# v_m times w1 for four batches in one matmul: two row halves, a doubled w1, and pieces moved by DMA

## The chip, the cores and the metric

One core of a Trainium2 chip runs the kernel. The metric is the device time of one execution in microseconds (us). The kernel before took 1427.96 us (median of 3 runs, 1426.88 to 1429.84).

The engines named below: PE is TensorE (matmuls, with their weight loads PEld), DVE is VectorE, ACT is ScalarE, POOL is GpSimd. SP is the queue on which this kernel issues its DMAs. Each engine works through its own instructions in order and waits where one needs another engine's result. A line such as L446 is a line of the kernel that was profiled.

## What is computed

A memory-compressed attention over 8 batches of 8 heads (576 positions, head size 64, 32 memory slots), then a mixture of 4 experts over all 4608 rows:

```python
a = exp(phi - max(phi)); a = a / (a.sum(over positions) + 1e-9)
k_m = einsum('bhsm,bhsd->bhmd', a, k)
v_m = einsum('bhsm,bhsd->bhmd', a, v)
attn = softmax(q @ k_m^T / sqrt(64))         # 576 x 32 for a head
x = (attn @ v_m) as 4608 rows x 512
p = domain_probs / (domain_probs.sum(-1) + 1e-9)
for e in range(4):
    out += p[:, e:e+1] * (relu(x @ w1[e]) @ w2[e])   # w1: 512 x 1024, w2: 1024 x 512
```

Everything is float32. The large matmuls run in a rounded format (fp32r). A number is split in two: its rounded part (a copy on ACT, which rounds) and the remainder (a subtraction on DVE or POOL). A product then takes three matmuls: rounded x rounded, rounded x remainder, remainder x rounded.

## The kernel before

**The product is reassociated.** attn @ v_m @ w1 is worked out as attn @ (v_m @ w1): for each batch and expert, the 8 heads' v_m (32 slots each, 256 rows in all) are multiplied by their 64 rows of w1, which gives a matrix called vw of 256 x 1024. It stands in SBUF as four tiles a batch, [128 rows, 2 parts, 512 columns]: `fh` (0, 1) is the half of the 1024 columns, `g` (0, 1) a group of four heads, 32 rows for each head, and the 2 parts are rounded and remainder. The first layer then has 256 rows to contract over instead of 512.

**Loops.** Batches go in pairs, k = 0 to 3. A pair goes through four experts, an expert through 32 steps: the even batch's positions in two halves (256 and 320 columns) of 8 steps each, then the odd batch's (320 and 256). A step s has `first(s)`, six matmuls of vw with the transposed attention weights AT into one PSUM tile, a relu on ACT (L427) and the remainder on DVE (L429); and `second(s)`, six or nine matmuls of that h with w2 (L445 to L447). `first` runs two steps ahead of `second`. A pair thus has 128 steps, the whole 512.

**A passage** from one expert to the next is spread over the last dozen steps of an expert. Four loads of w2 and four of w1 come into the `stage` buffers (5 of 512 KB), are split (`split`, L118 and L119, ACT and DVE) and, for w1, feed `vw_mm`: for each of eight (fh, head pair), three matmuls into a PSUM tile `pv` (L364 to L366), with `vt` as the stationary operand. `vt` holds a pair of batches' v_m laid out so that 128 output rows are 2 batches x 2 heads x 32 slots. `vw_out` takes them out of PSUM, for each batch half the rows: a cast on ACT (L379) and a subtraction on DVE (L380). So a passage has 24 matmuls of 512 columns, 16 casts and 16 subtractions for vw.

**Attention work** of a later batch is a list of units (`att_units`): normalise phi, turn it, split k and v (`unit_kv`, four loads), fold them to k_m and v_m (`kv_pick` into `kvT`), write v_m into `vt` (`write_vt`), then scores, softmax and the transposes to AT. The two batches of pair k + 1 are worked through during pair k.

**What sets the order.** A plan written out by hand gives the step of every unit (`W2_AT`, `W1_AT`, `VW_AT`, the `UNITS_` tables). The recording layer then puts each engine's instructions into an order of its own, by when it thinks that each is ready. All DMAs are issued from SP, in order; `stage_ahead` issues loads as stage buffers come free. DMAs share eight semaphores in turn, so one waits for the one eight places before it. PSUM has four buffers `pm` for first layers, pv and attention, and four `p2` for the second layer. The opening (up to the first steps) is ordered by hand.

## Time and profile before

| | |
|---|---|
| time, median of 3 runs | 1427.96 us |
| the profiled execution: its time | 1428.84 us |
| its span, first to last instruction | 1427.1 us |
| granted TensorE clock, mean | 0.996 |
| matmuls | 7808 |
| DMA, SP's queue | 113.86 MB, 24.5% of 16 engines' span |

The profile is of one execution. Its page gives for each engine the busy time, then the span in slices, the chain of work that ended last, and groups of like instructions: busy time, mean ns of one, the idle time just before them and what ended it. Other views list the waits (who waited for whom), the instructions in order of time, the busy time in chosen stretches, and the DMAs with the time from issue to landing. Matmuls overlap in the pipeline, so the listed duration of one (0.39 us for 512 columns) is longer than the distance to the next.

### The profile page before, as it was taken

How to read it: one execution, taken by the hardware profiler on the slowest of the kernel's cores; microseconds unless marked ns; L12 is line 12 of the kernel's file. 1: busy time of each engine (PE TensorE's matmuls, PEld its weight loads, DVE VectorE, ACT ScalarE, POOL GpSimd, SP SyncE). 2: the span in 40 equal slices, each digit the busy share in tenths (PEclk: the TensorE clock that was granted, in tenths of full speed). 3: DMA queues.
4: the chain of work that ended last, by engine and by line, in shares of the span. 5: the costliest groups of instructions: out<-in, count | busy, mean ns of one | idle time of the engine just before them, and what ended most of it. 6: DMA issues, size and time to landing. Idle time of an engine off the chain costs nothing.

```text
span 1427.1 us, 20830 instructions
## 1 busy us (share of the span) xinstructions
PE 1412.3 (99%) x7808; PEld 1233.5 (86%) x7808; DVE 837.2 (59%) x1853; ACT 620.2 (43%) x1543; POOL 27.8 (2%) x27
## 2 busy tenths in 40 slices
PE   7999999999999999999999999999999999999998
PEld 6888888888888888888888888888888888888887
DVE  7876638666385654837547375573846446272722
ACT  6655426453263533635335362452625234161521
POOL 3300000000000000000000000000000000000000
PEclk8999999999999999999999999999999999999999
DMA  6632303323141120412214121140323103030001
GB/s 245 198 118 75 121 28 126 104 64 104 39 161 61 64 89 16 137 58 78 94 63 135 59 88 65 46 130 18 107 75 96 60 25 94 1 119 1 1 30 38
DMA packets 35957, 115.20 MB, mean 81 GB/s; under 512 B 3984, under 2 KB 5136, under 8 KB 35856
## 3 DMA queue, kind: packets, MB, share of 16 engines
q1 hardware_dynamic: 35856, 113.86, 24.5%
q8 instruction: 62, 1.02, 0.3%
q14 instruction: 39, 0.32, 0.1%
HBM read 104.41 MB, written 9.44 MB: 80 GB/s over the span
## 4 chain that ended last, share of the span: by engine, by line
PE 92%; DMA 2%; DVE 2%; ACT 2%; issue 1%; POOL 0%; SPq 0%; ACTq 0%
PE p L446 18%; PE p L447 18%; PE p L445 18%; PE p L415 9%; PE p L417 9%; PE p L416 9%; PE sc L304 2%; PE pv L366 2%; PE pv L364 2%; PE x L230 2%; PE pv L365 2%; DMA stage<-in_w 1%; PE tp L349 1%; PE kvp L249 1%; ACT w L118 0%
## 5 line engine op out<-in xcount | busy, mean ns | idle before, releaser
L446 PE MATMUL p<-w,h 128*128 128x512 f32 x1024 | 404.3, 395 | 0.0
L447 PE MATMUL p<-w,h 128*128 128x512 f32 x1024 | 402.8, 394 | 0.0
L445 PE MATMUL p<-w,h 128*128 128x512 f32 x1024 | 402.7, 393 | 0.0
L427 ACT ACTIVATE h<-p 128x256 fp32r<-128x256 f32 x512 | 195.2, 382 | 331.5 <-PE p L417 294.3
L429 DVE SCALAR_TENSOR_TENSOR h<-p,h 128x256 fp32r<-128x256 f32 x512 | 213.9, 418 | 206.3 <-ACT h L427 110.0
L415 PE MATMUL p<-AT,vw 128*128 128x256 f32 (+1 forms) x1024 | 308.2, 301 | 0.0
L417 PE MATMUL p<-AT,vw 128*128 128x256 f32 (+1 forms) x1024 | 304.3, 297 | 0.1
L416 PE MATMUL p<-AT,vw 128*128 128x256 f32 (+1 forms) x1024 | 303.6, 297 | 0.0
L447 PEld LDWEIGHTS p<-w,h 128*128 128x128 f32 x1024 | 192.4, 188 | 43.3 <-DVE nm L154 0.2
L119 DVE TENSOR_TENSOR w<-stage,w 128x512 fp32r<-128x512 f32 x259 | 175.9, 687 | 78.4 <-ACT w L118 77.1
L445 PEld LDWEIGHTS p<-w,h 128*128 128x128 f32 x1024 | 193.2, 189 | 23.3
L446 PEld LDWEIGHTS p<-w,h 128*128 128x128 f32 x1024 | 192.6, 188 | 22.0
L416 PEld LDWEIGHTS p<-AT,vw 128*128 128x128 f32 x1024 | 194.5, 190 | 19.5 <-DVE AT L356 0.3
L415 PEld LDWEIGHTS p<-AT,vw 128*128 128x128 f32 x1024 | 194.0, 189 | 19.1
L417 PEld LDWEIGHTS p<-AT,vw 128*128 128x128 f32 x1024 | 193.5, 189 | 0.7 <-DVE vw L380 0.6
L118 ACT CAST w<-stage 128x512 fp32r<-128x512 f32 x262 | 159.6, 620 | 79.1 <-DMA stage<-in_w 47.3
L380 DVE TENSOR_TENSOR vw<-pv,vw 64x512 fp32r<-64x512 f32 x254 | 172.1, 685 | 8.9 <-ACT vw L379 5.5
L429 DVE SCALAR_TENSOR_TENSOR hm<-p,hm 128x64 fp32r<-128x64 f32 x256 | 56.0, 219 | 201.9 <-ACT h L427 200.9
L379 ACT CAST vw<-pv 64x512 fp32r<-64x512 f32 x254 | 145.5, 580 | 58.5 <-DVE vw L380 42.6
L427 ACT ACTIVATE hm<-p 128x64 fp32r<-128x64 f32 x256 | 56.6, 221 | 227.9 <-PE p L417 227.9
L462 DVE SCALAR_TENSOR_TENSOR acc<-p,pt,acc 128x512 f32<-128x512 f32 x96 | 67.8, 741 | 2.6 <-PE p L447 2.6
L366 PE MATMUL pv<-w,vt 128*128 128x512 f32 x136 | 53.7, 395 | 0.0
(81 smaller groups left out, 1020.5 us busy)
## 6 DMA issues: line engine op xcount, KB each, us to landing
stage<-in_w SPq DMA_DIRECT2D x132, 512.0 KB, 3.8
stage<-in_kv SPq DMA_DIRECT2D x32, 512.0 KB, 4.1
stage<-in_qm SPq DMA_DIRECT2D x16, 512.0 KB, 3.7
out<-acc SPq DMA_DIRECT2D x32, 256.0 KB, 2.1
ph<-in_phi SPq DMA_DIRECT2D x16, 288.0 KB, 3.5
stage<-in_kvt SPq DMA_DIRECT2D x8, 512.0 KB, 3.8
stage<-in_qt SPq DMA_DIRECT2D x8, 128.0 KB, 3.2
out<-accm SPq DMA_DIRECT2D x4, 256.0 KB, 2.2
```

Source lines behind the costliest of these rows:

```text
L118: nc.scalar.copy(dst[:, 0, :], raw)
L119: eng.tensor_sub(dst[:, 1, :], raw, dst[:, 0, :].bitcast(F32))
L379: nc.scalar.copy(t[r, 0, :], ps[r])
L380: nc.vector.tensor_sub(t[r, 1, :], ps[r], t[r, 0, :].bitcast(F32))
L415: nc.tensor.matmul(ps, w[:, 0, f], at_t[:, g, 0, c], start=g == 0, stop=False)
L416: nc.tensor.matmul(ps, w[:, 0, f], at_t[:, g, 1, c], start=False, stop=False)
L417: nc.tensor.matmul(ps, w[:, 1, f], at_t[:, g, 0, c], start=False, stop=g == 1)
L427: nc.scalar.activation(t[:, 0, to], ps[:, at_], AF.Relu)
L429: nc.vector.scalar_tensor_tensor(t[:, 1, to], ps[:, at_], 0.0, t[:, 0, to].bitcast(F32), ALU.max, ALU.subtract)
L445: nc.tensor.matmul(po[t], x[:, 0, :], w[:, 0, :], start=j == 0, stop=False)
L446: nc.tensor.matmul(po[t], x[:, 0, :], w[:, 1, :], start=False, stop=False)
L447: nc.tensor.matmul(po[t], x[:, 1, :], w[:, 0, :], start=False, stop=j == NJ - 1)
```

## The change

For two groups of four batches (n = 0: batches 0 to 3, n = 1: batches 4 to 7), vw of a whole group is made at once: for n = 0 only for expert 3, for n = 1 for all four experts (`FOUR`). That happens in five passages; in the five that would have made the same for the group's second pair, finished tiles are loaded instead; the other five passages stay.

- `unit_four` takes one load of `w1d`, a copy of w1 made on the host in which the 64 rows of a head stand twice, on both halves of the 128 partitions. For each of two heads: cast on ACT, remainder on POOL, two matmuls (rounded and remainder of w1) with `vs` as the stationary operand. `vs` has for each head the rounded v_m on the upper 64 rows and its remainder on the lower 64, with 4 batches x 32 slots as the 128 output rows. So one matmul sums two products, and the remainder x remainder product is added.
- The result of a head (128 rows, 512 columns) is cast on ACT and its remainder taken on DVE into a tile `vst` (3 buffers, shared with `kvs`). Its rows belong to four batches: four DMAs of 32 rows and 128 KB move them, two into the vw tiles of the group's first pair, two into DRAM tiles `vwd` for the second. 16 heads in a passage make 64 such pieces.
- `load_vw` brings the second pair's tiles back (8 loads of 512 KB in a passage), one pair later.
- A row block of vst must keep its place, so batch b takes head h in slot h ^ TURN[b % 4] (the host permutes the heads).
- `kvT` is replaced by four `kT` and a small `v`; `vt` is kept for batches 0 to 3 alone; `kv_pick`, `write_vt` copy in smaller pieces; `v_hi`, `write_vs` are new. The k and v of all of batches 4 to 7 are worked out in pair 1 (table `ATT`), where those of 6 and 7 were made in pair 2.
- Buffers: stage 5 to 4, w2 10 to 9, kvs 2 to 3.

```diff
-STAGE = 5
-KVS = 2
+STAGE = 4
+KVS = 3
+VW_LOAD_AT = ((18, 22), (26, 30))
+TURN = (0, 2, 1, 3)
+FOUR = (3, 0)
+FOUR_AT = ((23, 24, 25, 27), (28, 29, 31, 32))
...
+KV_STEPS = (5, 5, 6, 8, 9, 12, 15, 18, 21)
+EVEN, ODD = (0, 4, 4, 8, 11, 11), (0, 5, 5, 10, 12, 13)
+ATT = {
+    2: (0, 31, (69, EVEN)), 3: (0, 61, (99, ODD)),
+    4: (PAIR, 0, (37, EVEN)), 5: (PAIR, 30, (99, ODD)),
+    6: (PAIR, 60, (PAIR + 37, EVEN)), 7: (PAIR, 88, (PAIR + 99, ODD)),
+}
...
-    kvT = [const.tile([P, 2, NP, 2 * M], F32, name=f"kvT{i}") for i in range(2)]
-    for t in kvT:
+    kT = [const.tile([P, NP, 2 * M], F32, name=f"kT{i}") for i in range(4)]
+    vts = [const.tile([P, NP, 2, P], F32R, name=f"vt{i}") for i in range(2)]
+    for t in [vts[0].bitcast(F32)] + kT + [vts[1].bitcast(F32)]:
         nc.gpsimd.memset(t, 0.0)
...
     def kv_pick(b, g):
...
+        for w in (1, 0):
+            for i in range(2):
+                r, m = slice(64 * i, 64 * i + 64), slice(M * i, M * i + M)
+                lo = slice(2 * M + M * i, 2 * M + M * i + M)
+                a = slice(2 * g, 2 * g + 2)
+                dst = st["v", b][r, a] if w else kT[b % 4][r, a, m]
+                src = st["kvp", b, g][r, :, w]
+                (nc.vector.tensor_copy if i else nc.scalar.copy)(dst, src[:, :, m])
+                nc.vector.tensor_add(dst, dst, src[:, :, lo])
...
+    def write_vs(b):
+        if b % 4 == 0:
+            st["vs", b // 4] = att.tile([P, 2, 4, P], F32R, name="vs", tag="vs")
+        vs, (v, vh) = st["vs", b // 4], v_hi(b, None)
+        for h in range(4):
+            q = slot(b, h)
+            rq, c = slice(64 * (q % 2), 64 * (q % 2) + 64), slice(M * q, M * q + M)
+            x, hi = v[rq, :, q // 2, :], vh[rq, :, q // 2, :]
+            if q % 2 == 0:
+                nc.scalar.copy(vs[:64, :, h, c], hi.bitcast(F32))
+            else:
+                nc.vector.tensor_copy(vs[:64, :, h, c], hi.bitcast(F32))
+            nc.vector.tensor_sub(vs[64:, :, h, c], x, hi.bitcast(F32))
...
+    def unit_four(n, e, fh, hp):
+        def emit(raw):
+            g, vs = hp // 2, st["vs", n]
+            for i in range(2):
+                h = 2 * (hp % 2) + i
+                w = wp.tile([P, 2, 512], F32R, name="w1", tag="w1", bufs=4)
+                split(w, raw[:, i, :], nc.gpsimd)
+                ps = psum.tile([P, 512], F32, name="pv", tag="pm", bufs=4)
+                for a in range(2):
+                    nc.tensor.matmul(ps, vs[:, g, h, :], w[:, a, :], start=a == 0, stop=a == 1)
+                t = att.tile([P, 2, 512], F32R, name="vst", tag="kvs", bufs=KVS)
+                nc.scalar.copy(t[:, 0, :], ps)
+                nc.vector.tensor_sub(t[:, 1, :], ps, t[:, 0, :].bitcast(F32))
+                for b in range(4):
+                    odd, r = b % 2, slice(M * slot(b, h), M * slot(b, h) + M)
+                    if b < 2:
+                        to = vw_tile(2 * n, e, odd, fh, g)
+                    else:
+                        if h == 0:
+                            key = f"vwd{n}{e}{odd}{fh}{g}"
+                            vwd[2 * n + 1, e, odd, fh, g] = dram.tile([P, 2, 512], F32, name=key)
+                        to = vwd[2 * n + 1, e, odd, fh, g]
+                    nc.sync.dma_start(to[r].bitcast(F32) if b < 2 else to[r], t[r].bitcast(F32))
+        return ("w1d", e, fh, hp), emit
+
+    def load_vw(k, e, odd, fh):
+        for g in range(2):
+            key = (k, e, odd, fh, g)
+            nc.sync.dma_start(vw_tile(*key).bitcast(F32), vwd.pop(key))
...
+                four = ne >= FOUR[nk // 2]
                 n = 0
                 for fh in range(2):
-                    for g in range(2):
+                    for hp in range(NP if four and nk % 2 == 0 else 0):
+                        at(s + FOUR_AT[fh][hp], unit_four(nk // 2, ne, fh, hp))
+                    for odd in range(2 if four and nk % 2 else 0):
+                        at(s + VW_LOAD_AT[odd][fh], lambda a=(nk, ne, odd, fh): load_vw(*a))
+                    for g in range(0 if four else 2):
                         at(s + W1_AT[2 * fh + g], unit_w1(nk, ne, fh, g))
...
+        "w1d": c(
+            np.tile(moe_w1.reshape(E, NP, 2, D, 2, 512).transpose(0, 4, 1, 3, 2, 5), (1, 1, 1, 2, 1, 1))
+        ),
```

Three places show how the instructions move. All are in the passage from the third to the fourth expert of pair 0, the first that makes vw for four batches. The numbers are those of tiles.

SP's queue, before: the loads of that passage, w2 and w1, and then queries.

```order
L104 DMA stage_2930<-in_w2 128x1024
L104 DMA stage_3023<-in_w1 128x1024
L104 DMA stage_3096<-in_w2 128x1024
L104 DMA stage_3126<-in_w1 128x1024
L104 DMA stage_3152<-in_w1 128x1024
L104 DMA stage_3186<-in_qm 128x1024
```

SP's queue now, some way into the passage: the pieces of head 3 (vst_3278), the loads of w1d for heads 6 and 7 (stage_3303) and for 8 and 9, and the pieces of head 4 (vst_3319).

```order
L473 DMA vw_3214<-vst_3278 32x1024
L473 DMA vw_3216<-vst_3278 32x1024
L473 DMA vwd03000_3218<-vst_3278 32x1024
L473 DMA vwd03100_3220<-vst_3278 32x1024
L123 DMA stage_3303<-in_w1d 128x1024
L123 DMA stage_3311<-in_w1d 128x1024
L473 DMA vw_3322<-vst_3319 32x1024
L473 DMA vw_3324<-vst_3319 32x1024
L473 DMA vwd03001_3326<-vst_3319 32x1024
L473 DMA vwd03101_3328<-vst_3319 32x1024
```

The loads for later heads now stand behind the pieces of earlier ones on one queue; before, nothing stood between loads.

PE, before: a head pair's three matmuls for two batches (pv), between the six matmuls of a second layer and a first layer.

```order
L445 MATMUL p2_3148<-w2_2075,h_3111 128x512
L446 MATMUL p2_3148<-w2_2075,h_3111 128x512
L447 MATMUL p2_3148<-w2_2075,h_3111 128x512
L364 MATMUL pv_3176<-w1_3128,vt_123 128x512
L365 MATMUL pv_3176<-w1_3128,vt_123 128x512
L366 MATMUL pv_3176<-w1_3128,vt_123 128x512
L415 MATMUL p1_3194<-AT_966,vw_2350 128x256
L416 MATMUL p1_3194<-AT_966,vw_2350 128x256
```

PE now: the end of 18 matmuls of second layers (the last two are shown), heads 6 and 7 with two matmuls each for four batches, a first layer, and heads 8 and 9.

```order
L532 MATMUL p2_3299<-w2_2273,h_3366 128x512
L533 MATMUL p2_3299<-w2_2273,h_3366 128x512
L460 MATMUL pv_3388<-w1_3385,vs_404 128x512 x2
L460 MATMUL pv_3401<-w1_3398,vs_404 128x512 x2
L501 MATMUL p1_3411<-AT_1020,vw_2429 128x256
L502 MATMUL p1_3411<-AT_1020,vw_2429 128x256
L503 MATMUL p1_3411<-AT_1020,vw_2429 128x256
L501 MATMUL p1_3411<-AT_1020,vw_2489 128x256
L502 MATMUL p1_3411<-AT_1020,vw_2489 128x256
L503 MATMUL p1_3411<-AT_1020,vw_2489 128x256
L460 MATMUL pv_3432<-w1_3429,vs_404 128x512 x2
L460 MATMUL pv_3449<-w1_3446,vs_404 128x512 x2
```

Heads come in twos, and a step's second layer no longer stands between one pv and the next.

ACT now, where the casts of the load for heads 12 and 13 stand (stage_3383): they are ahead of a relu (h_3510) and of head 9's cast (vst_3452).

```order
L137 CAST w1_3477<-stage_3375 128x512
L137 CAST w1_3490<-stage_3375 128x512
L137 CAST w1_3537<-stage_3383 128x512
L137 CAST w1_3554<-stage_3383 128x512
L513 ACTIVATE h_3510<-p1_3503 128x256
L462 CAST vst_3452<-pv_3449 128x512
```

ACT before, at the like place: casts of vw, of weights and relus take turns.

```order
L379 CAST vw_3246<-pv_3276 64x512
L118 CAST w1_3315<-stage_3152 128x512
L427 ACTIVATE h_3291<-p1_3284 128x256
L379 CAST vw_3249<-pv_3276 64x512
L118 CAST w2_3215<-stage_3096 128x512
L379 CAST vw_3304<-pv_3300 64x512
```

What moved is that casts for heads some way ahead stand together in front of work that earlier heads need.

More of the change, by code (lines that the diff above doesn't have):

```diff
@@ L69, in body @@
 @with_exitstack
-def body(ctx: ExitStack, tc: tile.TileContext, qm, qt, kv, kvt, phi, prob, w1, w2, out):
+def body(ctx: ExitStack, tc: tile.TileContext, qm, qt, kv, kvt, phi, prob, w1, w1d, w2, out):
     nc = tc.nc
@@ L134, in emit @@
             for i in range(2):
-                t = wp.tile([P, 2, DM], F32R, name="w2", tag="w2", bufs=NJ + 2)
+                t = wp.tile([P, 2, DM], F32R, name="w2", tag="w2", bufs=NJ + 1)
                 split(t, raw[:, i, :], eng)
@@ L253, in kv_pick @@
     def kv_pick(b, g):
-        kvd = kvT[b % 2][:, :, 2 * g:2 * g + 2]
-        kvp = st["kvp", b, g].rearrange("p h w c -> p w h c")
-        for i in range(2):
-            r, m = slice(64 * i, 64 * i + 64), slice(M * i, M * i + M)
-            if i == 0:
-                nc.scalar.copy(kvd[r, :, :, m], kvp[r, :, :, m])
-            else:
-                nc.vector.tensor_copy(kvd[r, :, :, m], kvp[r, :, :, m])
-        for i in range(2):
-            r, m = slice(64 * i, 64 * i + 64), slice(M * i, M * i + M)
-            lo = slice(2 * M + M * i, 2 * M + M * i + M)
-            nc.vector.tensor_add(kvd[r, :, :, m], kvd[r, :, :, m], kvp[r, :, :, lo])
+        if g == 0:
+            st["v", b] = att.tile([P, NP, M], F32, name="v", tag="v", bufs=2)
+        for w in (1, 0):
[7 more added lines that the diff above has]
+                nc.vector.tensor_add(dst, dst, src[:, :, lo])
     def unit_kv(b, hp):
@@ L279, in unit_kv, with slot, v_hi, write_vt @@
         return ("kv", b, hp), emit
[L281 to L291 removed]
+    def slot(b, h):
+        return h ^ TURN[b % 4]
+    def v_hi(b, gs=slice(0, 2)):
+        if ("vh", b) not in st:
+            st["vh", b] = att.tile([P, NP, M], F32R, name="vh", tag="vh")
+        split = lambda t: t.rearrange("p (g a) m -> p g a m", g=2)
+        v, vh = split(st["v", b]), split(st["vh", b])
+        if gs is not None:
+            nc.scalar.copy(vh[:, gs], v[:, gs])
+        return v, vh
+    def write_vt(b, gs=slice(0, 2)):
+        v, vh = v_hi(b, None)
+        vt = vts[b // 2].rearrange("p (g a) s c -> p g a s c", g=2)
+        for h in range(4):
+            q = slot(b, h)
+            r, rq = (slice(64 * (i % 2), 64 * (i % 2) + 64) for i in (h, q))
+            dst = vt[r, gs, h // 2, :, M * q:M * q + M]
+            x, hi = v[rq, gs, q // 2, :], vh[rq, gs, q // 2, :]
+            if r == rq:
+                nc.scalar.copy(dst[:, :, 0, :], x)
+                hi = dst[:, :, 0, :]
+            else:
+                nc.vector.tensor_copy(dst[:, :, 0, :], hi.bitcast(F32))
+            nc.vector.tensor_sub(dst[:, :, 1, :], x, hi.bitcast(F32))
+    def write_vs(b):
+        if b % 4 == 0:
+            st["vs", b // 4] = att.tile([P, 2, 4, P], F32R, name="vs", tag="vs")
+        vs, (v, vh) = st["vs", b // 4], v_hi(b, None)
+        for h in range(4):
+            q = slot(b, h)
+            rq, c = slice(64 * (q % 2), 64 * (q % 2) + 64), slice(M * q, M * q + M)
[5 more added lines that the diff above has]
+            nc.vector.tensor_sub(vs[64:, :, h, c], x, hi.bitcast(F32))
     def tiles(t0):
@@ L297, in scores_mm @@
         nt, n = tiles(t0)
-        kvd = kvT[b % 2]
+        kvd = kT[b % 4]
         if hps[0] == 0:
@@ L474, in att_units, with write @@
         u += [unit_kv(b, hp) for hp in range(NP)]
-        u += [lambda: write_vt(b)]
+        def write():
+            v_hi(b)
+            if b < 4:
+                write_vt(b)
+            write_vs(b)
+        u += [write]
         u += [unit_scores(b, t0) for t0 in (0, 2, 4)]
@@ L626, in body @@
         probabilities()
+    v_hi(0)
+    write_vs(0)
     load_phi(1)
@@ L641, in slots @@
     def slots(a):
-        return np.stack([a[b] if b % 2 == 0 else a[b][[2, 3, 0, 1, 6, 7, 4, 5]] for b in range(B)])
+        heads = lambda b: [i ^ TURN[b % 4] for i in range(H)]
+        return np.stack([a[b][heads(b)] for b in range(B)])
     q, k, v, phi = slots(q), slots(k), slots(v), slots(phi)
```

77 lines of the change are left out of this document (34 added, 43 removed).

## The prediction

> **What bounds the kernel now.** I read the busy table of the page first, then the chain that ended last, then what TensorE (PE) waited for, and then stretches of the span.
>
> ```profile
> span 1427.1 us, 20830 instructions
> ...
> PE 1412.3 (99%) x7808; PEld 1233.5 (86%) x7808; DVE 837.2 (59%) x1853; ACT 620.2 (43%) x1543; POOL 27.8 (2%) x27
> ...
> PE 92%; DMA 2%; DVE 2%; ACT 2%; issue 1%; POOL 0%; SPq 0%; ACTq 0%
> ```
>
> PE is busy for 99% of the span and carries 92% of the chain. Busy alone doesn't say that PE sets the pace, so next come its waits (waiter, what it waited for, us in all, times, longest) and then two stretches (busy us of PE, weight loads, DVE, ACT, POOL, and last the clock and the DMA share), the opening and a passage from one expert to the next.
>
> ```profile
> PE x L230 <- DVE a L188: 2.7, 1, 2.7
> ...
> PE sc L304 <- PE x L233: 0.3, 1, 0.3
> ```
>
> ```profile
> 0.00:30.00 30.00, 21.30 (x120) 19.07 (x121) 21.57 (x43) 19.51 (x44) 14.11 (x17) 0.89 0.75 274
> 300.00:340.00 40.00, 40.00 (x225) 34.99 (x224) 31.24 (x59) 24.23 (x51) 0.00 (x0) 1.00 0.33 100
> ```
>
> The waits are the ends of a list of seven; the longest of all is 2.7 us. In the opening 30 us PE is busy for 21.3; in the passage it is busy for 40.00 of 40, while DVE has 31 us of work and ACT 24. After the opening, PE doesn't wait. So fewer matmuls shorten the span one for one, as long as no new wait appears.
>
> **What goes.** A matmul's listed duration overlaps its neighbours; its price is the distance between starts.
>
> ```profile
> 303.15 0.39 PE L365 MATMUL pv<-w,vt 128*128 128x512 f32 x1
> 303.38 0.40 PE L366 MATMUL pv<-w,vt 128*128 128x512 f32 x1
> 303.61 0.28 PE L415 MATMUL p<-AT,vw 128*128 128x256 f32 x1
> 303.73 0.28 PE L416 MATMUL p<-AT,vw 128*128 128x256 f32 x1
> ```
>
> That is 0.23 us for 512 columns (303.38 to 303.61) and 0.12 for 256. A passage now has 24 of the former. The change replaces two passages (2 x 24 = 48) by one with 16 heads x 2 = 32: 16 fewer, five times (last expert of the first four batches, all four of the others). 80 x 0.23 = **-18.4 us**.
>
> **The opening.** PE waits there, so longer chains count.
>
> ```profile
> L259 ACT COPY kvT<-kvp 64x128 f32<-64x128 f32 x16 | 4.1, 259 | 9.0 <-PE kvp L249 9.0
> ...
> L265 DVE TENSOR_TENSOR kvT<-kvT,kvp 64x128 f32<-64x128 f32 x32 | 9.1, 285 | 1.0
> L261 DVE COPY kvT<-kvp 64x128 f32<-64x128 f32 x16 | 4.7, 294 | 24.5 <-ACT kvT L259 24.4
> ...
> L291 DVE TENSOR_TENSOR vt<-kvT,vt 128x64 fp32r<-128x64 f32 x4 | 0.7, 223 | 0.3 <-ACT vt L290 0.3
> 8.71 1.27 POOL L219 TENSOR_TENSOR kvs<-stage,kvs 128x512 fp32r<-128x512 f32 x1 [6.52 <-ACT kvs L218]
> ```
>
> The pick of the second half had one copy on DVE (0.29) and two additions (0.57) ahead of the scores; now it has v and then k, six instructions of half the width, some 0.23 each by the 64-column row: 1.4, so 0.5 more. Two more subtractions for vt stand ahead of the maximum: 0.45. Together **+1.0 us** (between 0 and 2). Clearing three times the columns costs POOL about 2 us more, inside the 6.5 us that it idles before 8.71. The later small copies, and the k and v of batches 6 and 7 made one pair earlier, load DVE and ACT while PE has its slack of two steps; I cost them at nothing. If that cover fails, one step, 6 x 0.12 + 6 x 0.23 = 2.1 us, is the most that I would expect to see.
>
> So without any new wait: 1428.84 (the profiled execution, span plus 1.7 around it, 0.9 above the median of the runs shown) - 18.4 + 1.0 = 1411.4.
>
> **What is added: five windows.** In each, 16 heads go w1 half (ACT), remainder (POOL), two matmuls, cast (ACT), remainder (DVE), four pieces (SP's queue), and PE needs the first piece of the last head when the next expert begins. PE's order is the same in all five: head 6 stands 51 wide and 24 narrow matmuls after head 0 (14.6 us), head 7 0.46 later, head 8 1.64 after head 6, head 9 0.46 after that, and the last vw tile is wanted 113 wide, 78 narrow and 8 score matmuls after head 0, at 36.2 us. The durations that fill this, first of the engines:
>
> ```profile
> L119 POOL TENSOR_TENSOR w<-stage,w 128x512 fp32r<-128x512 f32 x3 | 3.8, 1287 | 6.2 <-ACT w L118 6.2
> ...
> L427 ACT ACTIVATE h<-p 128x256 fp32r<-128x256 f32 x512 | 195.2, 382 | 331.5 <-PE p L417 294.3 <-issue 32.9
> ...
> L379 ACT CAST vw<-pv 64x512 fp32r<-64x512 f32 x254 | 145.5, 580 | 58.5 <-DVE vw L380 42.6 <-PE pv L366 10.3
> ...
> L380 DVE TENSOR_TENSOR vw<-pv,vw 64x512 fp32r<-64x512 f32 x254 | 172.1, 685 | 8.9 <-ACT vw L379 5.5
> ...
> L118 ACT CAST w<-stage 128x512 fp32r<-128x512 f32 x262 | 159.6, 620 | 79.1 <-DMA stage<-in_w 47.3 <-PE p L447 28.6
> ```
>
> Then SP's issues (start, duration), two of a run and one alone, and the landings, over the whole span and, from the packets' row on, in the first 20 us alone:
>
> ```profile
> 2.12 0.43 SPq L104 DMA_DIRECT2D stage<-in_kvt  x1
> 2.59 0.43 SPq L104 DMA_DIRECT2D stage<-in_kv  x1
> ...
> 310.51 0.33 SPq L104 DMA_DIRECT2D stage<-in_qt  x1
> ```
>
> ```profile
> stage<-in_w SPq DMA_DIRECT2D x132, 512.0 KB, 3.8
> ...
> ph<-in_phi SPq DMA_DIRECT2D x16, 288.0 KB, 3.5
> ...
> out<-acc SPq DMA_DIRECT2D x32, 256.0 KB, 2.1
> ...
> DMA packets 2132, 6.72 MB, mean 336 GB/s; under 512 B 228, under 2 KB 356, under 8 KB 2132
> ...
> q1 hardware_dynamic: 2132, 6.72, 92.6%
> ...
> stage<-in_w SPq DMA_DIRECT2D x7, 512.0 KB, 7.5
> ```
>
> No row shows a DMA of 32 rows, so three prices have two ends each. *An issue*: 0.33 us by itself, 0.47 from start to start in a run (2.12 to 2.59); the pieces come in runs, so 0.47. *A piece's landing*: 2.1 (a write from SBUF) to 3.5 (a load of 288 KB); I take 2.8. *A load's landing*: 3.8, or 7.5 in the first 20 us, where the DMA engines are 92.6% busy at 336 GB/s, that is 363 at full share. A window moves 64 x 128 KB and some 8 loads of 512 KB, 12.6 MB: 35 us of the 36 by that rate, so a load won't land in 3.8 always; the queue isn't full from the start of a window, and I take 5, nearer to 3.8. Each DMA of the queue also waits for the one eight before it; eight issues take 3.8 us, so this binds only where landings are longer.
>
> A head's tile is ready 0.46 + 0.58 + 0.69 = 1.7 us after its matmuls begin; four pieces take SP 1.9. From head 0's matmuls: its pieces 1.7 to 3.6, head 1's to 5.5, a load to 6.0, head 2's to 7.9. There are three tile buffers, so head 3 waits for head 0's last piece (issued 3.1, landed 5.9), is ready at 7.2, and its pieces go out till 9.8. Only then SP issues the load for heads 6 and 7: landed 14.8, cast 15.4, POOL 16.7. PE wants it at 14.6: **2.1 late**. Head 7's remainder follows at 18.0 (0.8 late again), head 8's at 19.3 (0.1), head 9's at 20.6 (0.8): POOL makes one each 1.29 us, where PE's order has them in pairs. That is 3.8. Then the tail: the load for heads 12 and 13 needs the buffer of heads 6 and 7 (18.0), lands at 23.0, and its casts stand on ACT ahead of a relu and head 9's cast: 23.0 + 1.24 + 0.38 + 0.58 + 0.69 = 25.9. From there 28 pieces and 3 loads take 14.6 us, to 40.5; the last head's first piece went out at 38.6 and landed at 41.4, and PE wants it at 36.2 + 3.8 = 40.0: 1.4. **5.2 us a window, 26 in all: 1411.4 + 26 = 1437 us.**
>
> With the cheap ends (0.33, 2.1, 3.8) the load for heads 6 and 7 goes out at 8.1, the remainder is there at 13.8, and only the pairs cost, 0.9 a window: 1416. With the dear ends (0.47, 3.5, 7.5) head 6 is 4.6 late, the pairs cost 1.7, the tail 4.6, 10.9 in all: 1466. What is also dear: DVE's subtraction of two SBUF operands beside POOL.
>
> ```profile
> L614 DVE TENSOR_TENSOR w<-stage,w 128x512 fp32r<-128x512 f32 x2 | 2.2, 1135 | 0.0
> ```
>
> 1.135 us beside a busy POOL; there are eight such for w2 in a window, off the chain of heads, so I leave them in the range.
>
> The order speaks for waits too, though not for their length: before, each pv triple stands behind a plain step; now 18 matmuls of the second layer stand together ahead of head 6, which was not ready for an earlier place.
>
> **Rivals.** *The windows hold* (not slower). Place: the load for heads 6 and 7 behind 16 pieces. Price: 0.9 to 2.8 a window, 1416 to 1425. It decides at 3.5 a window, where 5 x 3.5 eats 17.4: with my landings, an issue of about 0.42 us. For it: one issue lasts 0.33 and a piece has a quarter of a load's rows. Against: DMA demand near the full rate.
>
> [...] If pieces move at half rate and one after another, a piece takes 128 KB at half of 418 GB/s, 0.63 us; 418 is the commonest full value in the opening 20 us, half a microsecond to a number:
>
> ```profile
> GB/s 0 0 0 111 115 383 364 371 295 336 189 156 164 336 352 401 426 418 418 401 451 410 418 418 418 434 410 401 418 410 410 377 399 398 388 413 415 395 410 410
> ```
>
> 64 x 0.63 + 8 loads x 1.25 = 50 us instead of 36; the last needed piece is three from the end, 1.7 + 50 - 1.9 + 2.1 = 52, so 16 late: 1411 + 80 = 1491. All transfers of this trace have 128 rows, so it neither shows nor excludes this. [...]
>
> *The change does not do what it says*: excluded by the order, which has 160 + 168 pv matmuls where there were 408.
>
> **Chances.** Forecast (waits of 3.9 to 11 a window): 0.37. Windows hold: 0.32. Between the two, within 0.2% (2.9 us, about what a measurement here can tell from no change): 0.13. Half rate: 0.18. So faster 0.32, same 0.13, slower 0.55. The range goes from 1414 (a little under the cheap end) to 1476 (over the dear end, leaving out most of the half-rate case).
>
> **What would show it.** In PE's waits after the change, pv of heads 6 to 9 behind POOL, or first layers behind DMA vw, five times, 3 to 6 us each time. Wrong would be: SP issues 0.33 to 0.42 us apart in the windows and loads landing under 4 us (windows hold); pieces landing in 4 us or more with issues waiting on earlier DMAs (half rate); PE waits outside the five windows (my zero for the moved attention work).

## The result, and the profile after

| | before | after |
|---|---|---|
| time, median (us) | 1427.42 (1426.48 to 1429.84, 4 runs) | 1568.05 (1564.17 to 1570.70, 4 runs) |
| ratio, 95% interval | | 1.0984 [1.0970, 1.0998] |
| span of the profiled execution (us) | 1427.1 | 1568.5 |
| mean granted TensorE clock | 0.996 | 0.953 |

Slower was right, by 10% instead of 0.6%: 1568 us against 1437 predicted, far above the range's end of 1476. The page of the changed kernel (busy time of the engines; PE and the granted clock in 40 slices; share of the chain that ended last):

```profile
PE 1455.6 (93%) x7728; PEld 1251.1 (80%) x7728; DVE 762.7 (49%) x1797; ACT 577.5 (37%) x1495; POOL 131.0 (8%) x111
...
PE   7999999978999999999977968977968999999999
...
PEclk8999999978999999999988978978978999999999
...
PE 83%; DMA 5%; DVE 4%; issue 3%; SPq 2%; ACT 2%; POOL 1%; DVEq 0%; POOLq 0%; ACTq 0%
```

PE dips at five places, the five windows, and its clock dips with it. 80 matmuls fewer, yet PE is busy for 43 us longer than the 1412.3 before. What PE waited for (waiter, what it waited for, us in all, times, longest):

```profile
PE pv L460 <- ACT w L137: 32.5, 10, 5.3
PE p L501 <- DMA vw<-vst: 13.8, 3, 7.8
...
PE p L501 <- DVE vst L463: 9.5, 4, 2.8
PE pv L460 <- POOL w L138: 8.3, 12, 0.9
```

Both waits that I named are there, but POOL's is the small one. The long ones are the copy of w1 that came late (ACT w) and the last heads' data at the start of the next expert (DMA vw, DVE vst).

In the second window the first head's matmuls start at 773.8. The matmuls of heads 6, 10 and 11, and the first layer that needs the last tile (start, duration, in brackets the wait before it):

```profile
792.83 0.79 PE L460 MATMUL pv<-w,vs 128*128 128x512 f32 x1 [4.28 <-ACT w L137]
...
804.21 0.50 PE L460 MATMUL pv<-w,vs 128*128 128x512 f32 x1 [1.71 <-ACT w L137]
805.56 0.80 PE L460 MATMUL pv<-w,vs 128*128 128x512 f32 x1 [0.85 <-POOL w L138]
...
837.26 0.55 PE L501 MATMUL p<-AT,vw 128*128 128x256 f32 x1 [7.75 <-DMA vw<-vst]
```

From head 0 to that first layer PE needs 63.5 us (773.8 to 837.26) for work that I put at 36.2. The same window in stretches (busy us of PE, weight loads, DVE, ACT, POOL; then the clock, the DMA share and GB/s):

```profile
774.00:786.00 12.00, 12.00 (x65) 10.29 (x64) 7.49 (x13) 5.88 (x13) 2.56 (x2) 1.00 0.73 199
788.50:792.50 4.00, 0.06 (x1) 0.00 (x0) 1.97 (x4) 1.93 (x4) 0.00 (x0) 0.93 0.94 305
792.50:798.50 6.00, 5.11 (x13) 3.56 (x14) 1.12 (x2) 2.90 (x6) 4.98 (x4) 0.50 0.93 272
798.50:802.50 4.00, 4.00 (x20) 3.06 (x18) 1.09 (x3) 1.49 (x3) 0.00 (x0) 0.97 0.84 246
802.50:806.00 3.50, 0.94 (x3) 0.63 (x3) 1.92 (x4) 3.18 (x6) 1.76 (x2) 0.94 0.54 133
806.00:809.50 3.50, 3.02 (x10) 1.91 (x10) 0.18 (x1) 0.59 (x2) 3.21 (x3) 0.57 0.87 238
```

Two things are to be seen. In five of the six stretches the DMA engines are 0.73 to 0.94 busy while they move 199 to 305 GB/s; the opening of before moved 336 at 0.926. And after PE has stood still for 4.28 us its clock is 0.50 over the next 6 us: 13 matmuls in 6 us, then 20 in 4.

The chain that ended last shows how a delay is handed on (start, duration, what; same window):

```profile
794.99 0.42 SPq L473
...
795.45 5.09 DMA stage<-in_w1d
...
804.24 1.28 POOL w L138
...
815.46 5.64 DMA stage<-in_w
821.12 0.62 ACT w L137
...
824.17 0.57 ACT vst L462
824.76 0.70 DVE vst L463
...
832.23 5.03 DMA vw<-vst
```

SP's pieces stand ahead of a load of w1d (5.09 us), which lands at 800.54. Its casts (heads 10 and 11, with those of 12 and 13 behind) start only 3 us later, because ACT has other casts ahead of them in its order; those of w2 had waited for matmuls of a second layer (L533), which were late themselves. ACT's casts of weights (start, duration of one or of four, in brackets the wait before them; the first two are of w2, the last four of w1d):

```profile
801.18 0.62 ACT L137 CAST w<-stage 128x512 fp32r<-128x512 f32 x1 [0.77 <-PE p L533]
...
802.54 0.62 ACT L137 CAST w<-stage 128x512 fp32r<-128x512 f32 x1 [0.26 <-PE p L533]
...
803.54 2.18 ACT L137 CAST w<-stage 128x512 fp32r<-128x512 f32 x4
```

The chain gives these 3 us to no one ("issue", 3.59 us before POOL). Later a load of w2 (5.64 us, `stage<-in_w`) holds up ACT, in whose order its cast stands ahead of a head's cast (vst), and that head's pieces are behind it again.

### The profile page after: what moved, and what is told of

Same layout as the page of the kernel before. It is cut to its first block, busy times and chain, and to the rows that moved or that the text cites. A ratio compares the mean times of both kernels' runs of the same rounds, so it can differ in the third digit from the quotient of the medians.

```text
span 1568.5 us, 21385 instructions
## 1 busy us (share of the span) xinstructions
PE 1455.6 (93%) x7728; PEld 1251.1 (80%) x7728; DVE 762.7 (49%) x1797; ACT 577.5 (37%) x1495; POOL 131.0 (8%) x111
## 4 chain that ended last, share of the span: by engine, by line
PE 83%; DMA 5%; DVE 4%; issue 3%; SPq 2%; ACT 2%; POOL 1%; DVEq 0%; POOLq 0%; ACTq 0%
PE p L531 16%; PE p L532 16%; PE p L533 16%; PE p L501 9%; PE p L503 8%; PE p L502 8%; PE sc L354 2%; SPq L473 2%; PE pv L460 2%; DMA stage<-in_w1d 2%; PE x L249 2%; DMA vw<-vst 1%; DMA stage<-in_w 1%; DVE vst L463 1%; PE pv L414 1%
## 5 line engine op out<-in xcount | busy, mean ns | idle before, releaser
L531 PE MATMUL p<-w,h 128*128 128x512 f32 x1024 | 411.4, 402 | 9.9 <-ACT h L513 9.9
L532 PE MATMUL p<-w,h 128*128 128x512 f32 x1024 | 409.1, 399 | 0.0
L533 PE MATMUL p<-w,h 128*128 128x512 f32 x1024 | 407.4, 398 | 0.7 <-DVE nm L173 0.7
L501 PE MATMUL p<-AT,vw 128*128 128x256 f32 (+1 forms) x1024 | 315.7, 308 | 33.8 <-DMA vw<-vst 13.8
L502 PE MATMUL p<-AT,vw 128*128 128x256 f32 (+1 forms) x1024 | 309.6, 302 | 0.8 <-DVE AT L406 0.8
L503 PE MATMUL p<-AT,vw 128*128 128x256 f32 (+1 forms) x1024 | 310.2, 303 | 0.2
L501 PEld LDWEIGHTS p<-AT,vw 128*128 128x128 f32 x1024 | 200.8, 196 | 57.5 <-issue 16.7
L533 PEld LDWEIGHTS p<-w,h 128*128 128x128 f32 x1024 | 195.9, 191 | 44.5 <-DVE nm L173 0.9
L531 PEld LDWEIGHTS p<-w,h 128*128 128x128 f32 x1024 | 196.5, 192 | 39.4 <-ACT h L513 14.7
L502 PEld LDWEIGHTS p<-AT,vw 128*128 128x128 f32 x1024 | 201.2, 196 | 21.3 <-DVE AT L406 1.3
L532 PEld LDWEIGHTS p<-w,h 128*128 128x128 f32 x1024 | 195.9, 191 | 23.0
L503 PEld LDWEIGHTS p<-AT,vw 128*128 128x128 f32 x1024 | 200.3, 196 | 0.8 <-DVE vw L435 0.5
L138 POOL TENSOR_TENSOR w<-stage,w 128x512 fp32r<-128x512 f32 x83 | 105.7, 1299 | 1006.2 <-ACT w L137 805.0
L138 DVE TENSOR_TENSOR w<-stage,w 128x512 fp32r<-128x512 f32 x179 | 122.7, 697 | 81.3 <-ACT w L137 79.3
L460 PE MATMUL pv<-w,vs 128*128 128x512 f32 x160 | 65.2, 505 | 48.6 <-ACT w L137 32.5
L460 PEld LDWEIGHTS pv<-w,vs 128*128 128x128 f32 x160 | 34.9, 231 | 71.5 <-ACT w L137 36.8
L463 DVE TENSOR_TENSOR vst<-pv,vst 128x512 fp32r<-128x512 f32 x80 | 53.3, 686 | 47.8 <-ACT vst L462 42.3
```

The source lines that it names most:

```text
L138: eng.tensor_sub(dst[:, 1, :], raw, dst[:, 0, :].bitcast(F32))
L460: nc.tensor.matmul(ps, vs[:, g, h, :], w[:, a, :], start=a == 0, stop=a == 1)
L463: nc.vector.tensor_sub(t[:, 1, :], ps, t[:, 0, :].bitcast(F32))
L501: nc.tensor.matmul(ps, w[:, 0, f], at_t[:, g, 0, c], start=g == 0, stop=False)
L502: nc.tensor.matmul(ps, w[:, 0, f], at_t[:, g, 1, c], start=False, stop=False)
L503: nc.tensor.matmul(ps, w[:, 1, f], at_t[:, g, 0, c], start=False, stop=g == 1)
```

## The experiments

Theories at the start: **A**, 32-row transfers hold the DMA engines longer than their bytes ask; **B**, SP's issues of 64 pieces set the pace; **D**, POOL's remainders in series; later **F**, the tail, from the last head to the next expert's first layer. In all runs "the change" is the changed kernel, of which one thing is altered. Where no number of runs stands beside a time, it is of one run.

### 1. Everything but the windows

```diff
-FOUR = (3, 0)
+FOUR = (4, 4)
```

(With a third `vt` tile, write_vt for all batches, and without write_vs.)

> Everything of the change but the four-batch passages: every expert's weights again by 24 narrow-row matmuls for each pair, the new order of the heads, the separate v tiles, the earlier attention work and the three kvs buffers stay. The recorded working (+1.0 us for the opening, nothing for the moved work): 1427 to 1431 us, like the kernel before. The rival that the moved attention work costs PE its slack: 2 us or more for each moved step, 1440 us and above.

**1438.26 us** (4 runs), ratio 1.0081 [1.0061, 1.0101] to 1426.57 before: +8.7 to +14.4 us, over the 1427 to 1431 expected, and not 1440 and above. The first matmul of the second layer starts at 36.38 us, 34.56 before: 1.8 us for the opening, within my 0 to 2 (the change itself has it at 36.57: 2.0). The other ten or so are spread over the run, with no single wait of PE over 2.2 us; whether the earlier attention work or the fewer buffers make them was not separated.

This gives a base for a window: 1438.3 - 18.4 = 1419.9 us without any window's cost. The price of a window in each run below is (its time - 1419.9) / 5; the change itself has 29.6 us.

### 2. The shape and the number of the transfers, and the tail

```diff
-                    odd, r = b % 2, slice(M * slot(b, h), M * slot(b, h) + M)
+                    odd, part, c = b % 2, h // 2, slice(256 * (h % 2), 256 * (h % 2) + 256)
...
-                    nc.sync.dma_start(to[r].bitcast(F32) if b < 2 else to[r], t[r].bitcast(F32))
+                    to = to[:, part, c]
+                    nc.sync.dma_start(to.bitcast(F32) if b < 2 else to, t[:, part, c].bitcast(F32))
```

> As the change, but each of a head's four pieces is a 128-row, 256-column block of one part of the tile instead of 32 rows of both parts: the same number of DMAs, the same 128 KB each, the same queue and order (the data lands in the wrong places, so the output is not the reference's). Theory A (32-row transfers hold the DMA engines longer than their bytes): the DMA share in the windows falls from 0.9 to about 0.75 at the same bytes, pieces land in 2 to 3 us, and the time falls to 1430-1470 us. Theory B (the issues on SP's one queue, four for a head at 0.58 us, set the pace): issues and time stay, 1545-1570 us.

**1501.18 us**, 16.3 a window: between the two theories, nearer to A's side in what it shows: same number of issues, the DMA share 0.72 in a window's stretch (755 to 790; 0.81 in the like stretch of the change, 773.8 to 809), and almost half of the cost gone. One sign of A did not come: the median landings are 3.7 and 2.9 us, not 2 to 3, and longer than the 3.3 and 2.5 of the change.

One DMA for a head (`b = h`, the whole tile t to one tile; the first pair's two tiles are those of heads 0 and 1 of each four):

> As the change, but one 128-row DMA of the whole 512 KB tile for each head instead of four pieces of 32 rows: a quarter of the DMAs, the same bytes (data in the wrong places, as in the run before). A and B both: no stall for pieces; 1411 plus what POOL's remainders cost, 1416-1425 us. Theory D (POOL's remainders of 1.3 us in series make most of a window's cost): 1500 us or more, with pv still behind POOL.

**1444.78 us**, 5.0 a window, 20 us over A and B's upper end, 8.5 of it the rest that the first run shows (1419.9 instead of 1411.4); far from D's 1500.

The same two with the last head's data needed first, as in the change:

```diff
-                b = h
+                b = 3 - h
```

> As the run with one 128-row DMA for a head, but in reverse: the last head of each four fills the first pair's even tile, which the next expert needs first (there it was the first head; data in the wrong places, as there). So PE again needs the last head's data at the start of the next expert, with 16 DMAs a window instead of 64. Theory F (the tail: last head, cast, remainder, transfer, first layer, is a large part of a window): 5 to 9 us more a window than with the first head, 1470-1490 us, with PE p waiting on DMA vw<-vst and the clock dropping there. If the tail is small (1.4 us a window, as the recorded working has it): 1445-1455 us.

**1480.72 us**, 12.2 a window: theory F as expected, 7.2 us more for nothing but the order. PE's waits of this run (the same columns as above):

```profile
PE p L499 <- DMA vw<-vst: 15.5, 4, 5.8
PE pv L460 <- POOL w L138: 10.4, 20, 1.1
```

```diff
-                    odd, part, c = b % 2, h // 2, slice(256 * (h % 2), 256 * (h % 2) + 256)
+                    odd, part, c = b % 2, (3 - h) // 2, slice(256 * ((3 - h) % 2), 256 * ((3 - h) % 2) + 256)
```

> As the run with pieces of 128 rows and 256 columns, but with the blocks in reverse, so that the first layers need the last head's pieces as they do in the change. Same number, bytes, queue and tail as the change; only the shape of a piece differs (data in the wrong places). Theory A (the 32-row shape costs): it stays near the 1501 us of the run before, under 1520. Theory F (its gain was the relaxed tail): 1540-1570 us.

**1502.59 us**, 16.5 a window: the gain of 128 rows is the shape's, not a relaxed tail's. So four kernels and the base make a ladder:

| step | time (us) | a window | the step's part |
|---|---|---|---|
| the change: 64 pieces of 32 rows, late tail | 1568.05 | 29.6 | |
| 64 pieces of 128 rows, late tail | 1502.59 | 16.5 | 13.1 shape |
| 16 DMAs of 128 rows, late tail | 1480.72 | 12.2 | 4.4 number and size |
| 16 DMAs of 128 rows, early tail | 1444.78 | 5.0 | 7.2 tail |
| no window (the first run, less 18.4) | 1419.9 | 0 | 5.0 the rest |

The third row has fewer DMAs, each four times as large and with whole rows, so its 4.4 us is not of the number alone. The parts hold for this order of steps; the three rows between are of one run each, and another order might share them out differently.

PE's busy rows of these kernels, from one late DMA for a head to 64 pieces of 128 rows, each of its own page:

```profile
PE 1424.0 (96%) x7728; PEld 1227.4 (83%) x7728; DVE 764.2 (52%) x1797; ACT 575.9 (39%) x1495; POOL 133.7 (9%) x111
```

```profile
PE 1435.9 (96%) x7728; PEld 1236.5 (82%) x7728; DVE 765.2 (51%) x1797; ACT 579.1 (39%) x1495; POOL 133.1 (9%) x111
```

and of the one with the early tail:

```profile
PE 1408.9 (98%) x7728; PEld 1216.3 (84%) x7728; DVE 763.2 (53%) x1797; ACT 575.7 (40%) x1495; POOL 134.0 (9%) x111
```

The same 7728 matmuls keep PE busy for 1408.9, 1424.0, 1435.9 and (the change) 1455.6 us, at mean clocks of 0.996, 0.982, 0.976 and 0.953. Of the 125.5 us of span between the first and the last, 46.7 are slower matmuls and 78.8 idle time: over a third of the price is the clock's. The clock by itself says the same: over stretches of 2 us, PE's busy time multiplied by what its clock lacks to 1 adds up to 52.3 us in the change and 4.6 in the kernel with the early tail, 47.7 more.

### 3. Bytes and issues

```diff
-                    nc.sync.dma_start(to[r].bitcast(F32) if b < 2 else to[r], t[r].bitcast(F32))
+                    nc.sync.dma_start(to[r, 0].bitcast(F32) if b < 2 else to[r, 0], t[r, 0].bitcast(F32))
```

(the first layers read part 0 twice, and the loads of `vwd` bring part 0 alone)

> As the change, but a piece carries only the rounded part of its 32 rows, 64 KB instead of 128, and the first layers read the rounded part in the place of the remainder: the same number of DMAs and the same rows, half the bytes. Theory A with a rate by bytes: DMA share in the windows near 0.6, landings under 3 us, 1430-1460 us. Theory B: issues stay at about 0.58 us each and the time at 1540-1570 us.

**1520.85 us**, 20.2 a window: half the bytes at the same number of pieces is worth 9.4 us a window. A's signs came (DMA share 0.62 in a window's stretch, 764 to 820; median landings 2.7 and 1.9 us), but not its time (1430 to 1460), and the time is under B's. Neither theory alone gives this.

```diff
-                for b in range(4):
+                for b in range(2):
```

> As the change, but the second pair's 32 pieces of each expert are left out, and its tiles are loaded from one DRAM tile written once (so the second pairs' outputs are wrong): SP issues 32 pieces a window instead of 64, some 23 us with the loads instead of 40, and the DMA engines move 8.4 MB instead of 12.6, 30 us at the 282 GB/s that full share gave in the window of the changed kernel. Both are under PE's 36 us. If issues and DMA time together make the cost: 1440-1455 us, as with one DMA for a head. If the 32-row copies from SBUF to SBUF alone are what is slow, whatever their number: landings of 3.3 us and more stay, and over 1480 us.

**1530.96 us**, 22.2 a window: a miss for both theories as I had put them, since half the issues and half of the pieces' bytes left three quarters of the cost. In this run the longest waits are the tail's (p on DMA vw: 16.1 us in three, up to 8.2), which it leaves in place. The other outcome, copies of 32 rows that are slow whatever their number, fits in its time (over 1480) but not in its sign: the median landing fell from 3.3 us to 2.7.

```diff
-                    nc.sync.dma_start(to[r].bitcast(F32) if b < 2 else to[r], t[r].bitcast(F32))
+                    q = nc.sync if b < 2 else nc.scalar
+                    q.dma_start(to[r].bitcast(F32) if b < 2 else to[r], t[r].bitcast(F32))
```

> As the change, but the second pair's 32 pieces are issued by ACT instead of SP. SP then issues for some 23 us a window, the DMA engines still carry 12.6 MB. Issues alone (theory B): 1440-1460 us. DMA time alone (theory A, 44.7 us at 282 GB/s against PE's 36): 1470 us or more, DMA share in the windows still 0.9. Rival for both: ACT stands in its order before each piece until DVE has made the remainder, so relu and casts come late: PE p <- ACT h grows from 9.9 us in all to over 40, 1540 us or more.

**1562.45 us**, 28.5 a window. Issues alone (1440 to 1460) are out. The rival's sign and its time (1540 or more) are there; A's bound (1470 or more) holds too, so the time doesn't tell these two apart. PE's longest waits:

```profile
PE p L532 <- ACT h L514: 41.6, 20, 5.1
PE pv L460 <- ACT w L137: 30.8, 11, 5.2
```

PE waits for the w1 copy as long as before (30.8 against 32.5), but now ACT comes late itself: its own waits for loads of w1d fell from 31.2 us in all to 9.9, while its casts of heads wait 33.5 us for the first pair's pieces (DMA vw<-vst; 0.3 in the change). The loads hardly go out sooner, the first 14.1 us after head 0's matmuls in the second window instead of 14.6, for they still stand behind pieces of heads that are late. The tail's wait (p on DMA vw) fell from 13.8 us to 0.8, and the one for relu grew from 9.9 to 41.6. So this run moves cost to ACT; it does not show that SP's issues cost nothing.

```diff
-            nc.sync.dma_start(t, src)
+            (nc.gpsimd if order[i][0] == "w1d" else nc.sync).dma_start(t, src)
```

> As the change, but the loads of w1d are issued by POOL, where they do not stand behind the pieces; SP keeps all 64 pieces. If the loads' place behind the pieces is the main part (PE pv <- ACT w is the longest wait of the changed kernel, 32.5 us): that wait falls under 10 us and the time to 1500-1530 us, while first layers still wait for the last pieces (64 x 0.58 = 37 us of issues). If POOL's issues are slow or stand before its remainders: PE pv <- POOL w over 20 us and no gain, 1560 us or more.

**1605.27 us**, 37.1 a window, the worst of all. The wait for the w1 copy fell to 9.5 us as foreseen, but no gain came of it: PE now waits for heads' tiles (p and pv on DVE vst: 27.1 and 21.3 us, against 9.5 and 7.6). The second outcome has the time (1560 or more) but not the reason: pv on POOL w is 6.2 us, not over 20. ACT's waits give a lead: its casts of weights now wait 35.6 us, in 19 places, for pv matmuls (L460), which the change does not have at all, and in ACT's order casts of heads and relus stand behind them. That this makes the heads late is not shown.

```diff
-                split(w, raw[:, i, :], nc.gpsimd)
+                split(w, raw[:, i, :], nc.vector)
```

> As the change, but w1d's remainders are made by DVE (0.69 us each) instead of POOL (1.29). Theory D (POOL's remainders in series are a main part): the waits of pv on POOL (8.3 us) go, the buffers come free earlier, 1500-1530 us. If DMA and SP set the pace: the time falls by less than 4 us a window, 1550-1568 us.

**1545.79 us**, 25.2 a window: POOL's place is worth 4.5 us a window, between the two expectations (1550 us and above, 1530 and below). PE's wait for the w1 copy stays at 32.4 us.

### 4. A piece by itself

The kernel before, with five sets of copies in its last 90 us, from a tile that POOL fills (`probe` at five steps; A and C 32 rows, E 64, B 128 x 256 columns, D 128 whole):

```diff
+            if kind == "B":
+                c = slice(256 * (i % 2), 256 * (i % 2) + 256)
+                nc.sync.dma_start(to[:, i % 4 // 2, c], src[:, i % 4 // 2, c])
+            elif kind == "D":
+                nc.sync.dma_start(to, src)
+            else:
+                n = 64 if kind == "E" else 32
+                r = slice(n * i % P, n * i % P + n)
+                nc.sync.dma_start(to[r], src[r])
```

> The kernel before, with five sets of copies from a tile in SBUF added in its last 90 us, where the queue is nearly empty: A 16 of 32 rows (128 KB) to SBUF, E 8 of 64 rows (256 KB) to SBUF, B 16 of 128 rows and 256 columns (128 KB) to SBUF, C 16 of 32 rows (128 KB) to DRAM, D 4 of 128 rows (512 KB) to SBUF. If 32 rows reach half of the paths: A and E land later than B and D for their bytes, and where the DMA engines are busy the rate at full share is near 200 GB/s in A and E against 360 to 410 in D. If a piece costs only its issue: A, B and C all run at 0.58 us a piece (226 GB/s), with landings of 2 to 2.5 us and a DMA share of 0.55 to 0.6 in each. Issue durations of all five are read too.

**1426.72 us** beside 1427.74 of the kernel before: the copies cost nothing there. A stretch inside each set, in the order A, E, B, C, D (the last two numbers are the DMA share and GB/s):

```profile
1348.00:1358.00 10.00, 10.00 (x59) 8.75 (x58) 3.77 (x7) 2.90 (x7) 0.00 (x0) 1.00 0.83 179
1368.00:1374.00 6.00, 6.00 (x34) 5.39 (x33) 1.40 (x6) 1.00 (x4) 0.00 (x0) 1.00 1.00 237
1386.00:1395.00 9.00, 9.00 (x48) 7.76 (x47) 1.67 (x6) 1.56 (x7) 0.00 (x0) 1.00 0.54 177
1409.00:1414.00 5.00, 5.00 (x30) 4.34 (x29) 1.12 (x3) 0.77 (x2) 1.18 (x2) 1.00 0.95 277
1416.00:1420.00 4.00, 4.00 (x22) 3.43 (x21) 0.43 (x1) 0.39 (x1) 0.00 (x0) 1.00 1.02 406
```

A and B move the same bytes at the same pace of issues, but A keeps the DMA engines 0.83 busy and B 0.54. At full share (GB/s over share): 216 for 32 rows to SBUF, 237 for 64 rows, 328 for 128 rows of 256 columns, 292 for 32 rows to DRAM, 398 for whole tiles. This shows theory A by itself: from SBUF to SBUF, 32 rows had 0.54 of the rate of whole tiles, and 64 adjacent rows hardly more (0.60). Set A goes over both halves of the rows in turn and stays at 216. The run shows the rates; what makes them is in no trace. To DRAM the loss was smaller: 32 rows (set C, over both halves in turn as well) had 0.73 of the rate of whole tiles, so the half of the pieces that goes to DRAM is not at half rate.

The issues of the sets A and B on SP, and the landings of all five:

```profile
1346.43 11.48 SPq L651 DMA_DIRECT2D pA<-src  x16
...
1383.66 11.29 SPq L645 DMA_DIRECT2D pB<-src  x16
```

```profile
pA<-src SPq DMA_DIRECT2D x16, 128.0 KB, 2.4
pE<-src SPq DMA_DIRECT2D x8, 256.0 KB, 4.9
pB<-src SPq DMA_DIRECT2D x16, 128.0 KB, 2.1
pC<-src SPq DMA_DIRECT2D x16, 128.0 KB, 2.6
pD<-src SPq DMA_DIRECT2D x4, 512.0 KB, 6.1
```

An issue takes 0.7 us from start to start in either shape (11.48 / 16), and a piece's landing alone tells little: 2.4 against 2.1.

Then 64 rows in the kernel, two pieces of 256 KB for a head:

```diff
-                for b in range(4):
-                    odd, r = b % 2, slice(M * slot(b, h), M * slot(b, h) + M)
+                for b in (1 - h % 2, 3 - h % 2):
+                    odd, r = b % 2, slice(64 * (1 - h // 2), 64 * (1 - h // 2) + 64)
...
-                        if h == 0:
+                        if h < 2:
```

> As the change, but two pieces of 64 adjacent rows (256 KB) for a head instead of four of 32: 32 DMAs a window instead of 64, the same bytes and the same tail; four pieces in a row lie on the same half of the rows (data in the wrong places). If adjacent rows of one half reach half of the paths: no gain from 64 rows, and worse for lying on one half, 1545-1590 us. If the number of rows in a DMA is what counts: between the 32-row kernel and the run with one late 128-row DMA (1481), 1500-1530 us.

**1555.03 us**, 27.0 a window: half the number of DMAs, the same bytes and tail, and 2.6 us of gain. That is in the range of the outcome in which 64 rows gain nothing (1545 to 1590), as set E's 237 GB/s beside A's 216 would have it; against B, and against "few rows in a DMA".

### 5. Two versions meant to be faster

Four-batch passages for the second four batches alone, 16 heads over 15 steps, the split of w1 two steps ahead:

```diff
-FOUR = (3, 0)
+FOUR = (4, 0)
-FOUR_AT = ((23, 24, 25, 27), (28, 29, 31, 32))
+FOUR_AT = (3, 5, 7, 9, 11, 13, 15, 17)
...
+                nc.sync.dma_start(vwd[e, fh, g][h], t.bitcast(F32))
...
+            d = vwd[e, fh, g].rearrange("h (s r) a c -> (h s) r a c", r=M)
+            nc.sync.dma_start(t[M * r:], d[r:5 * 3 - 4 * r + 1:5])
+            if r:
+                nc.sync.dma_start(t[:M * r], d[4 * (4 - r):16:5])
...
```

> A version meant to use less of what was short: four-batch passages only for the second four batches (64 matmuls fewer, -14.7 us), each head's tile goes to DRAM whole, in one DMA of 128 rows, and both pairs' tiles come back by 128-row loads (one or two each); the 16 heads are spread over 15 of an expert's 32 steps, and w1's split stands two steps ahead of its matmuls; batches 5 to 7 are made earlier. If issues (16 + 28 a passage instead of 64) and 32-row transfers made the cost: no window left, 1427 - 14.7 + 2 to 6 for the rest = 1414-1420 us, PE granted clock 0.996. If four-batch work itself has a price (POOL's remainders, the loads of w1 twice): 1 us or more for each of four passages, 1420-1435 us.

**1475.27 us** (4 runs), ratio 1.0338 [1.0317, 1.0358]: under the change, over before, and over both expectations. Its chain has DMAs that land late, at a mean clock of 0.985:

```profile
774.84 14.71 DMA stage<-in_w1d
...
825.23 11.98 DMA vwd<-vst
```

The loads from DRAM take their rows from one to four blocks of 32 that lie apart; what such a load costs by itself is not shown. The next run is the same with 32-row pieces to DRAM, in their final place, and plain loads of 128 rows:

```diff
-                nc.sync.dma_start(vwd[e, fh, g][h], t.bitcast(F32))
+                for b in range(4):
+                    r = slice(M * slot(b, h), M * slot(b, h) + M)
+                    nc.sync.dma_start(vwd[e, fh, g][b, r], t[r].bitcast(F32))
```

> The spread version again, but without the strided loads: each head goes out in four 32-row pieces of 128 KB, all to DRAM, over 15 of an expert's 32 steps, and every tile comes back in one load of 128 rows. If those strided loads of 3 or 4 blocks were what made the first spread version slow (a load of w1d beside them landed after 14.7 us): loads land in 4 to 5 us, PE waits in the four passages under 2 us each, 1416-1428 us. If the queue's order (loads behind pieces that wait for a head) is enough to make PE wait even at this spacing: 1440-1475 us as before.

**1457.00 us** (4 runs), ratio 1.0205 [1.0185, 1.0226]: the loads land in 5.4 to 5.6 us (median), where they took up to 14.7 in the chain above, and PE's longest wait in the passages is 2.1 us. But the time is in the range of the other outcome (1440 to 1475), although no long wait speaks for it. Many waits of about one microsecond or less remain, for relu, POOL and loads of q. From the first run less the 64 matmuls (1438.3 - 14.7 = 1423.6) some 33 us stay unexplained, eight a passage. Neither version beats the kernel before.

## Why the prediction failed, step by step

**The bound, and what goes.** PE set the pace before; the 80 matmuls are gone (7728 against 7808). The 18.4 us were not measured by themselves: the ladder's base takes them over, so if less was saved, its last part (5.0) is smaller by a fifth of the difference.

**The opening and the moved work.** +1.8 us in the opening against 1.0, within its range. "I cost them at nothing", of the moved attention work (and the buffers, which I did not cost at all), was wrong by some ten microseconds: the first run measures 11.7 in all. The 2.1 us that I called the most I would expect if the cover failed was too little as well.

**A window, 5.2 us.** This is the step that failed, by a factor of nearly six (29.6). Its place was right: five windows, pv behind the w1 copy from head 6 on, then the tail; outside them PE waits little. The inputs were nearly right too: the median landing is 5.0 us for a load of w1d (5 taken), 3.3 and 2.5 for pieces (2.8). These lines of the changed kernel show it:

```profile
stage<-in_w1d SPq DMA_DIRECT2D x40, 512.0 KB, 5.0
...
vw<-vst SPq DMA_DIRECT2D x160, 128.0 KB, 3.3
vwd<-vst SPq DMA_DIRECT2D x160, 128.0 KB, 2.5
```

What the recurrence made of them was not:

- *The issue*, 0.47 us, is about 0.6 in a window. The changed kernel's issues on SP in the second window (start, duration of the two in a row): pieces, the loads for heads 6 to 9 (`stage<-in_w1d`), and pieces again:

```profile
785.75 1.15 SPq L473 DMA_DIRECT2D vw<-vst  x2
786.94 1.41 SPq L473 DMA_DIRECT2D vwd<-vst  x2
788.39 0.91 SPq L123 DMA_DIRECT2D stage<-in_w1d  x2
790.60 1.15 SPq L473 DMA_DIRECT2D vw<-vst  x2
791.79 1.28 SPq L473 DMA_DIRECT2D vwd<-vst  x2
```

  The first of those loads goes out at 788.39, 14.6 us after head 0's matmuls, where I had 9.8; head 6 is 4.28 late instead of 2.1. The dearer issues of 16 pieces are some 2 us of that; most of the rest is three stores of the output that stood among the pieces (780.47 to 781.83), which were not in the recurrence, and a wait of 0.9 for head 3's tile. (The number of issues is a small part of the whole: pieces of 64 rows halve it for 2.6 us a window.)
- *The transfers* were counted at their bytes: 12.6 MB at 363 GB/s, 35 us of 36. At the probe's rates, 32 pieces at 0.61 us (128 KB at 216), 32 at 0.45 (at 292) and 8 loads at 1.32 (at 398) are 44 us: over the window. The ladder measures 13.1 us for the shape.
- *The tail*, 1.4 us, ends in a wait of 7.75 in the window shown, and its part is 7.2 a window where one DMA moves a head. I had the last head's piece land in 2.8; it lands in 5.03, with two stores, a load of w1d and four pieces issued in the 4 us before it. And w2's splits are not all "off the chain of heads": that was said of DVE's subtractions, but the cast of the same split holds ACT until its load has landed (5.64 us in the chain, then the cast of 0.62), and ACT's next cast is a head's.
- *The heads after 9* I had as never late. Heads 10 and 11 cost waits of 1.71 and 0.85 in the window shown. Their load had landed by then; it was ACT that came late, with casts of w2 and of heads ahead of theirs.
- *The clock* was in no term. The long waits also slowed the matmuls behind them: the clock is 0.50 over the 6 us behind the wait of 4.28, and 0.53 where PE goes on after that of 7.75 (837 to 843.5). Against the kernel with one early DMA for a head that makes 46.7 us over the five windows.

**The rivals.** The rival of half rate names the largest part (13.1 of 29.6 a window): the probe gives 0.61 us for a piece to SBUF where the rival had 0.63, though 0.45 for one to DRAM. But the change comes to 29.6 a window, not to its 16 (1491 us): it too lacked the clock, the casts behind loads, and the 11.7 us of the rest. I gave it 0.18 for lack of a row with 32 rows; the half was a supposition that no run shows as such, and the probe's rates for 32 rows are 0.54 (to SBUF) and 0.73 (to DRAM) of that of whole tiles. "The windows hold" was wrong, and its argument (a piece has a quarter of a load's rows) weighed the wrong thing, since in the probe the issue cost the same for 32 and 128 rows (0.7 us).

**What would show it.** "Pieces landing in 4 us or more" was a poor sign of half rate: the median landing is 3.3. The share of the DMA engines against what they move (0.93 at 272 GB/s) shows it at a glance.

## What to carry to other kernels

Price a small transfer by how long it holds the DMA engines, not by its landing when it is alone: share against GB/s in a stretch where the queue is full, for the very shape of rows that will be used (in the probe 32 and 128 rows landed in 2.4 and 2.1 us, but at full share they moved 216 and 328 GB/s). The window's demand came near its time (35 us of 36) and left its in-order queues no slack: loads behind pieces, casts behind loads, heads behind casts each handed the delay on (63.5 us in the window shown, where I had 36.2), so such a stage is to be costed as late, not as just fitting. And add the clock's price to every long wait of PE that is expected: here, waits of 4.28 and 7.75 us were followed by a clock of 0.50 and 0.53, and two shorter ones close together by 0.57.
